# Gates put into token order by a product on chip instead of a trip through DRAM, in a three-stage kernel whose instruction order is planned by hand

## Chip, core and metric

One core of a Trainium2 chip. The metric is the device time of one execution in microseconds, median over the runs shown.

## The reference, cut to what matters

```python
def reference(...):
    attn_out = _attn_ref(q, k, v)            # 4 batches, 8 heads, 576 tokens, 64 wide; 32 landmarks a head
    x = attn_out.transpose(0, 2, 1, 3).reshape(2304, 512)
    x = _moe_ref(x, ...)                     # router, one expert a token, gate_w[token] * (relu(x @ w1[e]) @ w2[e])
    return _moe2_ref(x, ...)                 # rms norm * rms_g, silu(xn @ w_gate) * (xn @ w_val) @ w_out

def _attn_ref(q, k, v):                      # Nystrom attention: out = A @ Z @ C @ v
    q_lm, k_lm = means of 18 neighbouring tokens
    A, Bm, C = sm(q, k_lm), sm(q_lm, k_lm), sm(q_lm, k)
    Z = Bm.T / (norm1 * norminf + 1e-6); six times Z = 2 * Z - Z @ Bm @ Z

def _moe_ref(x, expert_emb, tau, w1, w2):
    logits = (x / |x|) @ (expert_emb / |expert_emb|).T / tau
    expert_idx = argmax(logits); gate_w = softmax(logits)[expert_idx]
```

## The kernel before, in words

The work is one program with three stages that overlap. **Front** (`phaseA`): for each batch b, q and k are loaded (`load`, L241), turned (`turn`), summed into landmarks (`sums`, L267, on VectorE or, as a halving tree of adds, on GpSimd), and go through `crow`, `inverse` (L378), `arow`, `logits`, which ends with the batch's expert index (token `e0`), and `xtile`, which gives each token's sum of squares `ss`. **Expert** (`class Expert`): once `e0` is known the weights of that expert are loaded (`load`, L877, eight 512 KB tiles `raw` in five slots). `first` (L926) multiplies w1 by the low-rank factor, and `rows` evicts the result through ScalarE and VectorE. `hidden` (L960) makes the hidden rows in PSUM banks of which five are to be had; `relu` (L970 on ScalarE, L972 on VectorE) evicts them. `split` (L899, L902) makes f16 pairs of w2 from `raw`. `second` (L999) multiplies by w2; the last 64 tokens of a batch are folded by one product (`fold`, L1008, after a ScalarE copy at L1014), and `out` (L1029, L1033) stores rows to the DRAM tensor `yd`. **Last** (`phase3`): token tiles are read back from `yd` (`prep3`, L1260), normed, combined, transposed by DMA, and multiplied by w_gate, w_val (L1507) and w_out (L1482); these weights come through `W3` (loads of 512 KB at L1166, conversions on VectorE at L1182 to L1186, ScalarE at L1213).

All engines work through a fixed order. `Order` (L28) makes it while the program is written: each task is a generator that yields (engine, cost) or a wait; of the tasks that could go, the one with the earliest start (plus a penalty) is emitted, and its result counts as ready after its cost and the engine's `LAT`. For a DMA (`D`) that is the cost in the yield, 1.5 for an expert load, and 0.95 on top. On the chip every engine then runs its own list strictly in that order and waits on semaphores. Where PE would be idle in the front's plan, `warm` (L227) writes filler products on ones (L236) there. SP issues all DMAs but two.

The gates (`gates`, L804): a chain of small VectorE operations over all 20 columns (4 batches, 5 columns of 128 tokens; the fifth holds 64, in partitions 64 to 127) with one Exp gives `t`. The last stage needs the same values as [128, 18], tokens in tiles of 128 over the whole 2304. That relaying is done through DRAM by six DMAs on SP:

```python
    for b in range(B):
        nc.sync.dma_start(d[b, 0:512].rearrange("(c p) -> p c", p=128), g[:, b, 0:4])       # L848
    nc.sync.dma_start(d[:, 512:576].rearrange("b p -> p b"), g[64:128, :, 4])               # L849
    yield "D", 2.0
    nc.sync.dma_start(st["gam"], st["gd"].rearrange("(t p) -> p t", p=128))                 # L851
```

`embed` (L716) norms the eight expert embeddings in 17 VectorE operations on 8x1 and is added with rank -1 (ahead of all, L778); `inverse` waits for its result (`ent`) just ahead of the product `pen` (L478).

Of the kernel before, what the change touches and what calls it, by code (L numbers as in the profile page):

```python
# [27 lines left out]
class Order:  # L28
# [6 lines left out]

    LAT = dict(P=0.1, V=0.14, W=0.14, A=0.18, G=0.1, D=0.95)

# [41 lines left out]
    def run(self):  # L79
        while self.tasks:  # L80
            now = []
            before = self.tasks[:]
            for t in before:
                kind, arg = t[3]
                while kind in ("wait", "get", "beside", "mark"):
                    if kind == "mark":
                        pass
                    elif kind == "beside":
                        t[1] = t[4]
                    elif kind == "wait":  # L90
                        if arg not in self.tok:
                            break
                        t[1] = max(t[1], self.tok[arg])
                    else:
                        if not self.pool[arg]:
                            break
                        self.pool[arg].sort()
                        t[1] = max(t[1], self.pool[arg].pop(0))
                    t[3] = next(t[2], None)
                    if t[3] is None:  # L100
                        self.tasks.remove(t)
                        break
                    kind, arg = t[3]
                else:
                    costs = arg if len(kind) > 1 else (arg,)
                    _, e, c = min((self.at(e, t[1]) + c + self.pen.get(e, 0) * c, e, c) for e, c in zip(kind, costs))
                    now.append((self.at(e, t[1]), t[0], t, e, c))
# [38 lines left out]
def consts(tc, st):  # L146
    nc = tc.nc
# [25 lines left out]
    st["fold"] = con.tile([128, 64], F32, name="fold")  # L173
    nc.vector.tensor_tensor(out=st["fold"], in0=st["idn"][:, 0:64], in1=st["idn"][:, 64:128], op=ALU.add)
    st["oh"] = con.tile([128, B, 5, 8], F16, name="oh")
    st["WTb"] = st["p2"].tile([128, B, 2, 2, 64], F32, name="WTb")
# [11 lines left out]
def phaseA(tc, ctx, c2, I, st, Jobs):  # L188
# [13 lines left out]
    bufs = dict(q=2, k=2, v=1, kT=2, qT=3, ts=2, kq=4, ct=2, et=4, raw=5, w2p=6, Pt=1, hT=8, etp=4, y=2)  # L202
    R = Order(dict(bufs, ae=2, ce=2, big=1, t=NPT, m=NPM, n=0, r=RB, e=EB, x=1, y2=2, rows=2), dict(P=0.5, V=1.5, A=3.8, G=2.3, D=1.75), PEN)
    wes = [p1.tile([128, 2, 32], F32, name=f"We{i}") for i in range(2)]
# [36 lines left out]
    def load(b, hh, src):  # L241
        yield "get", src
        yield "D", 1.65
        t = T[src, b, hh] = sb([128, 18, 64], src)
        nc.sync.dma_start(t, I[src][b, 4 * hh:4 * hh + 4].rearrange("h (l j) d -> (h l) j d", j=18))
        R.sig(src, b, hh)

    def loadv(b):
        yield "get", "v"
        yield "D", 3.6  # L250
        t = T["v", b] = sb([128, 8, 5, 64], "v")
        nc.sync.dma_start(t[:, :, 0:4].rearrange("p h c d -> p h (c d)"), I["v"][b, :, 0:512, :].rearrange("h (s c) d -> s h (c d)", c=4))
        nc.sync.dma_start(t[0:64, :, 4], I["v"][b, :, 512:576, :].rearrange("h s d -> s h d"))
        R.sig("v", b)
# [12 lines left out]
    def sums(b, hh, i, src):  # L267
# [5 lines left out]
        g = T[src + "T", b, hh][:, :, -576:].rearrange("p e (l j) -> p e l j", j=18)  # L273
        yield ("VG", (1.45, 3.3)) if b < 2 else ("G", 3.3)
        if R.eng != "G":
# [102 lines left out]
    def inverse(b):  # L378
# [73 lines left out]
        V.tensor_copy(Y, pp) if R.eng == "V" else A.copy(Y, pp)  # L452
        R.put("t")
        yield "get", "t"
        yield "P", 0.44
        pwt = ps_t.tile([128, 2, 2, 32], F32, name="pwt", tag="t")
        for g in range(2):
            bd = bdm[:, g].rearrange("p (a c) l -> p c a l", c=2)
            for c in range(2):
                nc.tensor.matmul(pwt[64 * c:64 * c + 64, g], lhsT=Y[:, g], rhs=bd[:, c], start=True, stop=True)  # L460
        yield "get", "t"
        yield "P", 0.38
        pw = ps_t.tile([128, 2, 64], F32, name="pw", tag="t")
        for g, h in heads:
            nc.tensor.matmul(pw[h, g], lhsT=Bm[h, g], rhs=Y[h, g], start=True, stop=True)
        WTb = st["WTb"][:, b]
# [4 lines left out]
        R.sig("WTb", b)  # L471
        yield "wait", ("ent",)
        yield "get", "t"
# [8 lines left out]
        R.put("t")  # L482
        R.sig("W", b)
        for g in range(2):
            yield "beside", 0
            yield "V", 0.41
            W = T["W", b, g] = sb([128, 256], "W", 4)
            V.tensor_tensor(out=W.rearrange("p (h d) -> p h d", h=4), in0=bc(pw[:, g], [128, 4, 64], "out"), in1=bc(icm[:, g], [128, 4, 64], "in"), op=ALU.mult)
# [208 lines left out]
    def pair(b):  # L697
# [4 lines left out]
        for hh in range(2):  # L702
# [6 lines left out]
            R.sig("etp", b, hh)  # L709
        yield "D", 0.7  # L710
        nc.sync.dma_start(st["ed"][b], tp)
        yield "wait", ("WTb", b)
        yield "D", 0.4
        nc.sync.dma_start(st["wd"][b], st["WTb"][:, b])
# [62 lines left out]

    R.add(embed(), -1)  # L778
    for b in range(B):
# [24 lines left out]
def gates(tc, R, st):  # L804
# [38 lines left out]
    V.tensor_tensor(out=t.rearrange("p (b c) -> p b c", b=B), in0=t.rearrange("p (b c) -> p b c", b=B), in1=bc(st["rsx"], [128, B, 5], "in"), op=ALU.mult)  # L843
    yield "D", 2.0
    g = t.rearrange("p (b c) -> p b c", b=B)
    d = st["gd"].rearrange("(b s) -> b s", b=B)
    for b in range(B):
        nc.sync.dma_start(d[b, 0:512].rearrange("(c p) -> p c", p=128), g[:, b, 0:4])  # L848
    nc.sync.dma_start(d[:, 512:576].rearrange("b p -> p b"), g[64:128, :, 4])  # L849
    yield "D", 2.0  # L850
    nc.sync.dma_start(st["gam"], st["gd"].rearrange("(t p) -> p t", p=128))  # L851
    yield "W", 0.18
# [4 lines left out]
class Expert:  # L857
# [19 lines left out]
    def load(self, b):  # L877
# [4 lines left out]
        for m in (1, 2):  # L882
            src = self.I[f"moe_w{m}"][bass.ds(e0, 1)].rearrange("a (k p) f -> p (a k) f", p=128)
            for k in range(4):
                yield "get", "raw"
                yield "D", 1.5
                raw = T["raw", m, b, k] = self.tile("raw", [128, m, 1024 // m], F32)
                nc.sync.dma_start(raw, src[:, m * k:m * k + m])
                R.sig("raw", m, b, k)
# [118 lines left out]
    def fold(self, b, pz):  # L1008
# [5 lines left out]
        nc.scalar.copy(y, pz)  # L1014
        R.put("m")
        yield "get", "m"
        yield "P", 0.85
        pz = self.ps.tile([128, 512], F32, name="pz", tag="m")
# [4 lines left out]
    def out(self, b, c, pz, r0, n):  # L1023
# [6 lines left out]
        R.put("m")  # L1030
        yield "D", 0.73
        t0 = 576 * b + 128 * c
# [213 lines left out]
def prep3(nc, R, stg, st, p):  # L1246
# [6 lines left out]
    def load(k):  # L1253
# [3 lines left out]
        yield "get", "y2"  # L1257
        yield "D", 0.73
        y = ys[k] = stg.tile([128, 512], F32, name="y2", bufs=2)
# [26 lines left out]
    for j in range(h):  # L1286
# [22 lines left out]
        for a in range(2):  # L1309
            yield "D", 1.57  # L1310
            nc.sync.dma_start_transpose(out=st["xT"][XT[p]][:, a, :, 128 * j:128 * j + 128], in_=rows[a].rearrange("p o d -> p (o d)"))
            R.put("rows")
# [25 lines left out]
def phase3(tc, ctx, I, st, out, stg, w3, R=None):  # L1338
# [86 lines left out]
    def last(p, t, g, po):  # L1425
# [15 lines left out]
        if g < 5:  # L1441
            return
        yield "D", 0.73
        n = PT[p][t]
# [74 lines left out]
def loads(R, w3):  # L1519
    while w3.nload < len(w3.jobs):  # L1520
        yield "get", "r"
        yield "D", 1.46
        w3.load()
# [10 lines left out]
def build(tc, I, out):  # L1534
    nc = tc.nc
    with ExitStack() as ctx:
# [6 lines left out]
        st["yd"] = dr.tile([NT, DM], F32, name="yd")  # L1543
        st["gd"] = dr.tile([NT], F32, name="gd")
        st["wd"] = dr.tile([B, 128, 2, 2, 64], F32, name="wd")
# [69 lines left out]
```

## Time and profile before

| | us |
|---|---|
| median of 3 runs | 719.98 (718.86 to 722.33) |
| the profiled execution | 716.13 |
| its span, first to last instruction | 714.4 |
| mean granted TensorE clock | 0.99 of full |
| PE busy | 682.7 |
| VectorE (DVE) busy | 456.0 |
| ScalarE (ACT) busy | 365.2 |
| GpSimd (POOL) busy | 69.6 |

Busy times are of the one profiled execution, and shares of them are averages over stages. The clock is given as a share of 2.4 GHz. An engine's idle time before an instruction is written in brackets with what released it.

### The profile page before, as it was taken

The numbers are of one execution on the slowest core, as the hardware profiler recorded it, in microseconds if no ns is written. First come the engines' busy times: TensorE is split into PE (matmuls) and PEld (weight loads), VectorE is DVE, ScalarE is ACT, GpSimd is POOL, SyncE is SP. The second block draws the span as 40 slices with busy tenths as digits, with TensorE's granted clock in tenths as the row PEclk, the third lists the DMA queues.
The fourth block names the chain that finished last, engine by engine and source line by source line (L and its number), as shares of the span: only waits on it lengthen the run. The fifth ranks groups of instructions, "written<-read, shape, count | busy, mean of one in ns | idle before, by whom it ended". The sixth has DMA issues, their size and how long they took to land. (4 is left out here: it accounts for less than half of the span.)

```text
span 714.4 us, 14850 instructions
## 1 busy us (share of the span) xinstructions
PE 682.7 (96%) x5996; PEld 474.7 (66%) x5996; DVE 456.0 (64%) x1071; ACT 365.2 (51%) x851; POOL 69.6 (10%) x89
## 2 busy tenths in 40 slices
PE   9989999999679998998999999999999999999994
PEld 9867677655424545466777777777777777777882
DVE  8997886735578887878887955456554543344331
ACT  1335775636446957566466554454544443333431
POOL 0025571010110301000000100000000000000000
PEclk9999999999889999999999999999999999999998
DMA  8255807435776885466313220452422030000101
GB/s 300 94 187 196 269 9 250 141 115 158 126 229 189 241 220 174 147 173 156 108 33 116 89 61 1 96 126 76 115 54 68 18 95 1 1 1 2 61 1 35
DMA packets 70142, 80.91 MB, mean 113 GB/s; under 512 B 42920, under 2 KB 47528, under 8 KB 70064
## 3 DMA queue, kind: packets, MB, share of 16 engines
q1 hardware_dynamic: 70032, 79.86, 38.7%
q8 instruction: 49, 0.80, 0.5%
q14 instruction: 29, 0.24, 0.1%
q10 hardware_dynamic: 32, 0.02, 0.0%
HBM read 59.27 MB, written 12.33 MB: 100 GB/s over the span
## 5 line engine op out<-in xcount | busy, mean ns | idle before, releaser
L1482 PE MATMUL po<-w_out,u 128*128 128x512 f16 x648 | 157.5, 379 | 0.7 <-ACT u L1412 0.5
L1507 PEld LDWEIGHTS <-w_gate 128*128 128x128 f16 x1260 | 114.0, 98 | 35.6 <-issue 2.0
L1507 PEld LDWEIGHTS <-w_val 128*128 128x128 f16 x1260 | 113.5, 98 | 13.0 <-issue 1.5
L1482 PEld LDWEIGHTS <-u 128*128 128x128 f16 x648 | 62.7, 98 | 55.8 <-ACT u L1412 1.5
L1385 DVE SCALAR_TENSOR_TENSOR cgate<-ps_gateb,cgate 128x256 f32<-128x256 f32 x81 | 34.2, 422 | 97.6 <-ACT cgate L1382 94.7
L1507 PE MATMUL ps_gatea<-x,w_gate 128*128 128x256 f16 (+1 forms) x720 | 88.6, 262 | 0.0
L1507 PE MATMUL ps_vala<-x,w_val 128*128 128x256 f16 (+1 forms) x720 | 88.6, 262 | 0.0
L999 PE MATMUL pz<-w2p,hT 128*128 128x512 f16 x384 | 86.8, 380 | 0.0
L1382 ACT ACTIVATE cgate<-ps_gatea 128x256 f32<-128x256 f32 x81 | 31.0, 382 | 96.9 <-PE ps_gatea L1507 96.4
L999 PEld LDWEIGHTS <-hT 128*128 128x128 f16 x384 | 36.0, 98 | 49.3 <-issue 5.7
L1507 PE MATMUL ps_gateb<-x,w_gate 128*128 128x256 f16 (+1 forms) x540 | 66.4, 262 | 1.3 <-DVE cgate L1385 1.3
L1507 PE MATMUL ps_valb<-x,w_val 128*128 128x256 f16 (+1 forms) x540 | 66.4, 262 | 1.0 <-DVE cval L1385 0.7
L960 PE MATMUL ph<-etp,Pt 128*128 128x288 f16 x384 | 52.3, 293 | 6.1 <-DVE hT L972 6.1
L1412 ACT CAST u<-cval 128x512 f16<-128x512 f32 x54 | 33.3, 616 | 41.6 <-DVE cval L1391 22.4
L960 PEld LDWEIGHTS <-Pt 128*128 128x128 f16 x384 | 37.9, 100 | 17.6 <-issue 6.6
L1416 DVE TENSOR_TENSOR u<-cval,u 128x512 f16<-128x512 f32 x54 | 37.3, 691 | 16.2 <-ACT u L1412 14.1
L1391 DVE TENSOR_TENSOR cval<-cval,cgate 128x256 f32<-128x256 f32 x81 | 35.3, 436 | 8.7 <-ACT cgate L1388 1.0
L1382 ACT ACTIVATE cval<-ps_vala 128x256 f32<-128x256 f32 x81 | 31.0, 383 | 16.7 <-PE ps_vala L1507 16.5
L1385 DVE SCALAR_TENSOR_TENSOR cval<-ps_valb,cval 128x256 f32<-128x256 f32 x81 | 34.0, 420 | 8.6 <-ACT cval L1382 8.0
L1388 ACT ACTIVATE cgate<-cgate 128x256 f32<-128x256 f32 x81 | 33.5, 413 | 4.8 <-DVE cgate L1385 4.6
L972 DVE SCALAR_TENSOR_TENSOR hT<-ph,hT 128x288 f16<-128x288 f32 x64 | 27.3, 450 | 6.8 <-ACT hT L970 6.1
L970 ACT ACTIVATE hT<-ph 128x288 f16<-128x288 f32 x64 | 25.1, 409 | 10.5 <-PE ph L960 9.8
(224 smaller groups left out, 936.3 us busy)
## 6 DMA issues: line engine op xcount, KB each, us to landing
raw<-moe_w SPq DMA_DIRECT2D x32, 512.0 KB, 5.2
y<-yd SPq DMA_DIRECT2D x36, 256.0 KB, 3.4
r<-moe_w_gate SPq DMA_DIRECT2D x12, 512.0 KB, 4.6
r<-moe_w_val SPq DMA_DIRECT2D x12, 512.0 KB, 3.7
r<-moe_w_out SPq DMA_DIRECT2D x12, 512.0 KB, 3.6
k<-k SPq DMA_DIRECT2D x8, 576.0 KB, 4.9
q<-q SPq DMA_DIRECT2D x8, 576.0 KB, 5.4
out<-o SPq DMA_DIRECT2D x18, 256.0 KB, 2.0
```

The source lines that it names most:

```text
L960: nc.tensor.matmul(ph, lhsT=P[:, g, a, 128 * j:128 * j + 128], rhs=x[:, g, c, 288 * n:288 * n + 288], start=(q == 0), stop=(q == 5))
L970: nc.scalar.activation(h[:, 0, sl], ph, AF.Relu)
L972: nc.vector.scalar_tensor_tensor(out=h[:, 1, sl], in0=ph, scalar=0.0, in1=h[:, 0, sl], op0=ALU.max, op1=ALU.subtract)
L999: nc.tensor.matmul(pz, lhsT=h[:, a, s0:s0 + n], rhs=w[:, e, i], start=(j == 0 and q == 0), stop=(j == 6 and q == 5))
L1382: return lambda: (start(nm) if (i, h) == (1, 0) else None, A.activation(c[nm][:, i, h], banks[nm + ab][:, 0:m], AF.Copy, scale=C))
L1385: return lambda: V.scalar_tensor_tensor(out=c[nm][:, i, h], in0=banks[nm + "b"][:, 0:m], scalar=C, in1=c[nm][:, i, h], op0=ALU.mult, op1=A ...
L1388: return lambda: A.activation(c["gate"][:, i, h], c["gate"][:, i, h], AF.Silu)
L1391: return lambda: either(nc, R).tensor_tensor(out=c["val"][:, i, h], in0=c["val"][:, i, h], in1=c["gate"][:, i, h], op=ALU.mult)
L1412: A.copy(u[0][:, 0, i], c["val"][:, i].rearrange("p h m -> p (h m)"))
L1416: return lambda: either(nc, R).tensor_tensor(out=u[0][:, 1, i], in0=c["val"][:, i].rearrange("p h m -> p (h m)"), in1=u[0][:, 0, i], op=AL ...
L1482: nc.tensor.matmul(po[t], lhsT=u2[:, a, i, 128 * s:128 * s + 128], rhs=wo[:, b, i], start=(first and i == 0 and j == 0), stop=(final and i ...
L1507: nc.tensor.matmul(o, lhsT=wt[:, a, kk, w, 128 * (g % 2):128 * (g % 2) + 128], rhs=xT[:, b, 2 * x + kk, 0:m], start=(first and q == 0), st ...
```

## The change

Six things: the gates are relaid by one product with a matrix that swaps the halves of the partitions, and five VectorE copies, so that the six DMAs and `gd` are gone; `embed` has the rank of `inverse` and a penalty; `inverse` waits for `ent` ahead of `pwt` and makes `pw` after `We`; one landmark sum (batch 0, second half, q) goes to GpSimd; the planner counts a DMA's landing as 1.6 instead of 0.95, with higher costs for most DMAs; and `fold` gets a lag of 1.0 in the plan and a cost of 0.5 instead of 0.85.

```diff
-    LAT = dict(P=0.1, V=0.14, W=0.14, A=0.18, G=0.1, D=0.95)
+    LAT = dict(P=0.1, V=0.14, W=0.14, A=0.18, G=0.1, D=1.6)
...
+                    elif kind == "lag":
+                        t[1] += arg
...
+    st["swap"] = con.tile([128, 128], F32, name="swap")
+    for h in range(2):
+        nc.vector.tensor_copy(st["swap"][:, 64 * h:64 * h + 64], st["idn"][:, 64 - 64 * h:128 - 64 * h])
...
-    R = Order(dict(bufs, ...), dict(P=0.5, V=1.5, A=3.8, G=2.3, D=1.75), PEN)
+    R = Order(dict(bufs, ...), dict(P=0.5, V=1.5, A=3.8, G=2.3, D=0.2), PEN)
...
-        yield "D", 1.65
+        yield "D", 1.89
...
-        yield ("VG", (1.45, 3.3)) if b < 2 else ("G", 3.3)
+        yield ("G", 3.3) if b > 1 or (b, hh, src) == (0, 1, "q") else ("VG", (1.45, 3.3))
...
+        yield "wait", ("ent",)
         yield "get", "t"
         yield "P", 0.44
         pwt = ps_t.tile([128, 2, 2, 32], F32, name="pwt", tag="t")
...
-        yield "get", "t"
-        yield "P", 0.38
-        pw = ps_t.tile([128, 2, 64], F32, name="pw", tag="t")
-        for g, h in heads:
-            nc.tensor.matmul(pw[h, g], lhsT=Bm[h, g], rhs=Y[h, g], start=True, stop=True)
...
-        yield "wait", ("ent",)
...
         R.sig("W", b)
+        yield "get", "t"
+        yield "P", 0.38
+        pw = ps_t.tile([128, 2, 64], F32, name="pw", tag="t")
+        for g, h in heads:
+            nc.tensor.matmul(pw[h, g], lhsT=Bm[h, g], rhs=Y[h, g], start=True, stop=True)
...
-    R.add(embed(), -1)
+    R.add(embed(), PR["inv"], dict(W=0.2, V=0.2))
...
-    yield "D", 2.0
-    g = t.rearrange("p (b c) -> p b c", b=B)
-    d = st["gd"].rearrange("(b s) -> b s", b=B)
-    for b in range(B):
-        nc.sync.dma_start(d[b, 0:512].rearrange("(c p) -> p c", p=128), g[:, b, 0:4])
-    nc.sync.dma_start(d[:, 512:576].rearrange("b p -> p b"), g[64:128, :, 4])
-    yield "D", 2.0
-    nc.sync.dma_start(st["gam"], st["gd"].rearrange("(t p) -> p t", p=128))
+    yield "get", "m"
+    yield "P", 0.2
+    ps = st["ps_m"].tile([128, n], F32, name="psw", tag="m")
+    nc.tensor.matmul(ps, lhsT=st["swap"], rhs=t, start=True, stop=True)
+    g, h = [x.rearrange("p (k o c) -> p k o c", k=2, o=2) for x in (t, ps)]
+    o = st["gam"].rearrange("p (k c) -> p k c", k=2)
+    for to, fr in ((o[:, :, 0:4], g[:, :, 0, 0:4]), (o[64:128, :, 8:9], g[64:128, :, 1, 4:5]), (o[0:64, :, 4:5], h[0:64, :, 0, 4:5]),
+                   (o[64:128, :, 4:8], h[64:128, :, 1, 0:4]), (o[0:64, :, 5:9], h[0:64, :, 1, 0:4])):
+        yield "V", 0.16
+        V.tensor_copy(to, fr)
+        yield "beside", 0
+    R.put("m")
...
-                yield "D", 1.5
+                yield "D", 1.71
...
+        yield "lag", 1.0
         yield "get", "m"
-        yield "P", 0.85
+        yield "P", 0.5
...
-        yield "D", 0.73
+        yield "D", 0.85
...
-        yield "D", 1.46
+        yield "D", 1.71
```

The other costs of DMAs that change: v 3.6 to 3.78, `ed` 0.7 to 1.80, `wd` 0.4 to 0.36, the transposes of `prep3` 1.57 to 1.80; the stores and loads of `yd` and of the output all go from 0.73 to 0.85.

## Rows read from the trace of the kernel before

**Rows 1.** The page, part 1: busy time, share of the span and instructions.

```profile
PE 682.7 (96%) x5996; PEld 474.7 (66%) x5996; DVE 456.0 (64%) x1071; ACT 365.2 (51%) x851; POOL 69.6 (10%) x89
```

**Rows 2.** Stretches: length, busy PE, PEld, DVE, ACT, POOL, clock, DMA share, GB/s.

```profile
180.00:200.00 20.00, 14.24 (x85) 8.63 (x83) 9.78 (x22) 6.91 (x18) 0.39 (x1) 0.83 0.73 129
200.00:220.00 20.00, 15.96 (x67) 6.03 (x65) 17.32 (x42) 12.75 (x23) 2.40 (x3) 0.91 0.78 240
...
360.00:400.00 40.00, 40.00 (x304) 29.51 (x302) 34.41 (x72) 24.55 (x57) 2.83 (x3) 1.00 0.16 54
```

**Rows 3.** PE's timeline: start, us, what; in brackets the idle time before.

```profile
181.09 6.04 PE L960 MATMUL ph<-etp,Pt 128*128 128x288 f16 x48 [0.20 <-DVE hT L972]
192.69 4.48 PE L960 MATMUL ph<-etp,Pt 128*128 128x288 f16 x18 [5.56 <-DVE hT L972]
197.10 2.37 PE L926 MATMUL pP<-raw,WTb 128*64 128x512 f32 x8
199.40 1.47 PE L999 MATMUL pz<-w2p,hT 128*128 128x512 f16 x6
204.91 3.68 PE L926 MATMUL pP<-raw,WTb 128*64 128x512 f32 x8 [4.04 <-DVE Pt L936]
...
244.19 1.94 PE L926 MATMUL pP<-raw,WTb 128*64 128x512 f32 x8
```

**Rows 4.** ScalarE's timeline: the two splits of w2 that waited for a load.

```profile
189.96 1.06 ACT L899 ACTIVATE w2p<-raw 128x1024 f16<-128x1024 f32 x1 [6.05 <-DMA raw<-moe_w]
...
201.51 1.06 ACT L899 ACTIVATE w2p<-raw 128x1024 f16<-128x1024 f32 x1 [5.33 <-DMA raw<-moe_w]
```

**Rows 5.** SP's timeline: DMA issues around the gates.

```profile
180.41 0.39 SPq L888 DMA_DIRECT2D raw<-moe_w  x1
181.88 2.10 SPq L848 DMA_DIRECT2D gd<-gt  x4
...
192.30 0.39 SPq L888 DMA_DIRECT2D raw<-moe_w  x1
```

**Rows 6.** DMA issues: count, KB each, median us to landing, whole span.

```profile
raw<-moe_w SPq DMA_DIRECT2D x32, 512.0 KB, 5.2
...
gd<-gt SPq DMA_DIRECT2D x4, 2.0 KB, 11.3
```

**Rows 7.** The same view for the stretch 180 to 181 us alone.

```profile
raw<-moe_w SPq DMA_DIRECT2D x1, 512.0 KB, 9.5
```

**Rows 8.** A stretch inside the first stall; columns as in rows 2.

```profile
187.00:190.00 3.00, 0.13 (x2) 0.00 (x0) 0.00 (x0) 0.04 (x1) 0.00 (x0) 1.00 0.29 21
```

**Rows 9.** VectorE's timeline near the end of the gates' chain.

```profile
175.28 0.43 DVE L1182 TENSOR_SCALAR e<-r 128x512 int32<-128x512 int32 x1 [1.71 <-DMA r<-moe_w_gate]
...
181.69 0.16 DVE L843 TENSOR_TENSOR gt<-gt,rsx 128x20 f32<-128x20 f32 x1
```

**Rows 10.** VectorE's timeline in the first 20 us.

```profile
4.67 2.22 DVE L263 STREAM_TRANSPOSE kT<-k 128x1152 f32<-128x1152 f32 x1 [1.69 <-DMA k<-k]
6.75 0.15 DVE L730 TENSOR_SCALAR r8i<-ess 8x1 int32<-8x1 int32 x1
...
17.69 0.15 DVE L737 TENSOR_TENSOR r8t<-r8t,ess 8x1 f32<-8x1 f32 x1
17.87 1.35 DVE L276 TENSOR_REDUCE lm<-qT 128x64 f32<-128x1152 f32 x1
```

**Rows 11.** GpSimd's timeline: first and last rows of one landmark sum.

```profile
63.42 1.31 POOL L282 TENSOR_TENSOR ts<-kT 128x576 f32<-128x576 f32 x1 [5.24 <-DVE ev L663]
...
66.57 0.37 POOL L287 TENSOR_TENSOR lm<-ts 128x64 f32<-128x64 f32 x1
```

**Rows 12.** PE groups by line, 20 to 100 us: busy us, mean ns, idle before.

```profile
L236 PE MATMUL w<-ones 128*128 128x128 f16 x194 | 12.9, 219 | 0.0
```

**Rows 13.** PE's timeline: the third fold.

```profile
271.41 1.07 PE L1019 MATMUL pz<-y,fold 128*64 128x512 f32 x2 [2.48 <-ACT y L1014]
```

**Rows 14.** ScalarE's timeline just ahead of that fold's copy.

```profile
270.16 0.63 ACT L1269 ACTIVATE y<-y 128x512 f32<-128x512 f32 x1 [3.96 <-DMA y<-yd]
```

More of the change, by code (lines that the diff above doesn't have):

```diff
@@ L84, in run @@
                 kind, arg = t[3]
-                while kind in ("wait", "get", "beside", "mark"):
+                while kind in ("wait", "get", "beside", "mark", "lag"):
                     if kind == "mark":
                         pass
+                    elif kind == "lag":
+                        t[1] += arg
                     elif kind == "beside":
@@ L202, in phaseA @@
     bufs = dict(q=2, k=2, v=1, kT=2, qT=3, ts=2, kq=4, ct=2, et=4, raw=5, w2p=6, Pt=1, hT=8, etp=4, y=2)
-    R = Order(dict(bufs, ae=2, ce=2, big=1, t=NPT, m=NPM, n=0, r=RB, e=EB, x=1, y2=2, rows=2), dict(P=0.5, V=1.5, A=3.8, G=2.3, D=1.75), PEN)
+    R = Order(dict(bufs, ae=2, ce=2, big=1, t=NPT, m=NPM, n=0, r=RB, e=EB, x=1, y2=2, rows=2), dict(P=0.5, V=1.5, A=3.8, G=2.3, D=0.2), PEN)
     wes = [p1.tile([128, 2, 32], F32, name=f"We{i}") for i in range(2)]
@@ L249, in loadv @@
         yield "get", "v"
-        yield "D", 3.6
+        yield "D", 3.78
         t = T["v", b] = sb([128, 8, 5, 64], "v")
@@ L483, in inverse @@
         R.sig("W", b)
+        yield "get", "t"
[3 more added lines that the diff above has]
+            nc.tensor.matmul(pw[h, g], lhsT=Bm[h, g], rhs=Y[h, g], start=True, stop=True)
         for g in range(2):
-            yield "beside", 0
+            if g:
+                yield "beside", 0
             yield "V", 0.41
@@ L709, in pair @@
             R.sig("etp", b, hh)
-        yield "D", 0.7
+        yield "D", 1.80
         nc.sync.dma_start(st["ed"][b], tp)
         yield "wait", ("WTb", b)
-        yield "D", 0.4
+        yield "D", 0.36
         nc.sync.dma_start(st["wd"][b], st["WTb"][:, b])
@@ L843, in gates @@
     V.tensor_tensor(out=t.rearrange("p (b c) -> p b c", b=B), in0=t.rearrange("p (b c) -> p b c", b=B), in1=bc(st["rsx"], [128, B, 5], "in"), op=ALU.mult)
-    yield "D", 2.0
-    g = t.rearrange("p (b c) -> p b c", b=B)
-    d = st["gd"].rearrange("(b s) -> b s", b=B)
-    for b in range(B):
-        nc.sync.dma_start(d[b, 0:512].rearrange("(c p) -> p c", p=128), g[:, b, 0:4])
-    nc.sync.dma_start(d[:, 512:576].rearrange("b p -> p b"), g[64:128, :, 4])
-    yield "D", 2.0
-    nc.sync.dma_start(st["gam"], st["gd"].rearrange("(t p) -> p t", p=128))
+    yield "get", "m"
[8 more added lines that the diff above has]
+        V.tensor_copy(to, fr)
+        yield "beside", 0
+    R.put("m")
     yield "W", 0.18
@@ L1257, in load @@
         yield "get", "y2"
-        yield "D", 0.73
+        yield "D", 0.85
         y = ys[k] = stg.tile([128, 512], F32, name="y2", bufs=2)
@@ L1309, in prep3 @@
         for a in range(2):
-            yield "D", 1.57
+            yield "D", 1.80
             nc.sync.dma_start_transpose(out=st["xT"][XT[p]][:, a, :, 128 * j:128 * j + 128], in_=rows[a].rearrange("p o d -> p (o d)"))
@@ L1442, in last @@
             return
-        yield "D", 0.73
+        yield "D", 0.85
         n = PT[p][t]
@@ L1543, in build @@
         st["yd"] = dr.tile([NT, DM], F32, name="yd")
-        st["gd"] = dr.tile([NT], F32, name="gd")
         st["wd"] = dr.tile([B, 128, 2, 2, 64], F32, name="wd")
```

## The prediction

> **What bounds the kernel now.** The first view is the page's busy time: PE works 96% of the span [rows 1], so the end is set by PE's list, and a gain must come from PE's idle time, from its slow clock or from its filler products. The second view cuts the span into stretches: PE is busy all the time in the last stage (360 to 400 us is one such stretch, and it stays so to the tail), but from 180 to 220 us it has only 14.24 and 15.96 of 20 us, at a granted clock of 0.83 and 0.91 [rows 2]. That is the worst place behind the start. The third view is PE's timeline there: a stall of 5.56 us ahead of 192.69 and one of 4.04 ahead of 204.91 [rows 3]; between and behind them PE ran on the lower level (1.2 GHz) for a time, seen in the durations: eight L926 products took 3.68 us at 204.91 and 1.94 at 244.19 on the full clock. The bracket names VectorE as releaser, but VectorE waits for ScalarE, and ScalarE's timeline gives the root: two splits of w2 stood 6.05 and 5.33 us for an expert load [rows 4], and everything behind them in ScalarE's list, the relus that free PSUM banks included, stood too. Then SP's timeline: those loads were issued at 180.41 and 192.30, around the four gate stores at 181.88 [rows 5]. An expert load lands after 5.2 us in the median, a gate store of 2 KB takes 11.3 [rows 6]; the load of 180.41 took 9.5 [rows 7], the other 201.51 - 192.30 = 9.2. Between 187 and 190 us the DMA engines moved 21 GB/s, while all four engines stood still [rows 8]. I read this as stores of single four-byte values that clog the rings.
>
> **The gates' stores and load go.** From the end of the 48 L960 products (181.09 + 6.04 = 187.13) to the end of the second L926 (204.91 + 3.68 = 208.59) PE took 21.46 us. Its work in there at full clock is 18 x 6.04/48 = 2.27 for L960, 2 x 1.94 for L926 and 1.47 for L999, together 7.6 [rows 3]. So 13.8 us is the most that can be gained. If the order stays and only the landings fall to 5.2 us: the first load lands at 185.6 instead of 189.96, so its slot frees 4.35 earlier and the second is issued at 187.95; that one lands at 193.15 instead of 201.51, 8.4 us earlier, and the second L926 with it. If its clock stays up too, 3.68 - 1.94 = 1.74 more: 10.1. The new plan counts 1.71 + 1.6 = 3.31 us from issue to landing where it counted 1.5 + 0.95 = 2.45, so it puts a split 0.86 us further behind in ScalarE's list; I add that and take **-11.0**, between 8.4 and 13.8. On SP six issues go, four of them 2.10 us together [rows 5].
>
> The row that speaks against this is the issue time: the first late load went out 1.5 us ahead of the stores and was late all the same. The Trainium skill, DMA: Bandwidth & Descriptors, section Queues, rings and completion order, says that each DMA engine takes descriptors in the order of its ring. By that rule the stores could not hold up a load ahead of them, the first stall would stay, and the sum would be that of the first rival below. Against it stands the 21 GB/s of [rows 8]: had a backlog of large loads been the cause, the engines would have moved much more. I take the stores as the cause of both.
>
> **What comes in their place.** One f32 product over 20 columns on PE. The fold is the nearest row: 1.07 us for 512 columns [rows 13]; so between 0 and 1.07, and I take **+0.4**, as most of its columns are missing. It waits for the end of the gates' chain (181.69 + 0.16 [rows 9]), and behind it in PE's list stand the L960 products of batch 1; for those wait the relus. Five copies on VectorE at 0.16 each [rows 9], 0.8 us together, lie where VectorE had 9.78 us of work in 20 [rows 2], so nothing; without that cover they hold up the relu subtractions behind them by 0.8. The swap matrix is two copies at the start, in the 1.69 us in which VectorE waits for the first k [rows 10]: nothing, or 2 x 0.15 by the same short rows if that load came first.
>
> **The head.** Seven of the 17 embedding operations stand between the turns and sums of the first 20 us, the first at 6.75, the last at 17.69, where VectorE is full; each costs its 0.15 and a gap, up to 0.18 (17.69 to 17.87) [rows 10]: 7 x 0.18 = 1.2 us off VectorE's list. At their new rank they fill places where VectorE waits. The sum that goes to GpSimd frees 1.35 us on VectorE [rows 10] and takes 63.42 to 66.94, 3.5 us, there [rows 11]; the landmark comes 3.5 - 1.35 - 1.2 = about 1 us later, but VectorE can turn the next k meanwhile. PE has 12.9 us of fillers between 20 and 100 us [rows 12], so PE waits for this chain, and what VectorE gains there can reach the end. Bounds: +1 (the late landmark decides) and -2.55; I take the embeddings whole and half of the sum, **-1.9**. Putting `pw` behind `We` moves products and adds none: zero; its cover is the same filled stretch, and without it `W` comes late by that one group of products.
>
> **The fold and the longer landings.** The third fold stood 2.48 us [rows 13], because ScalarE ahead of its copy stood 3.96 for a token load [rows 14]. A lag of 1.0 in the plan lets other products go ahead by about that much: between 0 and -2.48, I take **-1.0**. In the rest of the order longer landings move instructions that wait for loads back; I count nothing, with one stall of the size of [rows 13], 2.5 us, either way.
>
> **Sum.** -11.0 + 0.4 - 1.9 - 1.0 = -13.5 us against the profiled execution: 716.1 to 702.6. The median of the runs is 3.9 us above that execution, and the difference should carry over: 719.98 - 13.5 = **706.5**. What a measurement of this kernel can tell from no change is about 0.5%, 3.6 us.
>
> **Rivals.** *Ring order: only the second load was late by the stores.* Then the first stall stays, the second load gains 9.2 - 5.2 = 4.0 and the clock 1.74: -5.7 + 0.4 - 1.9 - 1.0 = -8.2, 711.8. For it: the issue time; against it: [rows 8]. Chance 0.12.
>
> *VectorE becomes the bound ahead of the last stage.* PE comes 13.5 us sooner to the products with w_gate and w_val, while VectorE is at 34.41 of 40 us from 360 to 400 [rows 2] with the weights' conversions. Spare there is 14%; over the 150 us from 210 to 360 that is 21 us, more than 13.5, so it decides only where the spare lies in the wrong places. I price it at half the gain: 719.98 - 6.7 = 713.2. Chance 0.10.
>
> *The loads are late by themselves.* If neither stall came from the stores, the first term is zero: 0.4 - 1.9 - 1.0 = -2.5, 717.5. Against it: of 32 loads these two are far over the median [rows 6, 7]. Chance 0.05.
>
> *PE waits for the gates (slower).* The product stands in PE's list, and the chain ahead of it on VectorE shares its list with conversions that wait for weight loads: 1.71 us at 175.28 is one of three such conversions [rows 9]. Before, PE ran past that; now it stands there. If three loads came as late as the latest one here, 9.5 against 5.2, PE would stand 3 x (9.5 - 5.2) = 12.9 plus the 1.71 of the row and, as after 192.69, run 18 L960 products at half clock for 4.48 - 2.27 = 2.2 more: 16.8, and the gates' term of 11.0 is then no gain either, since the loads are as late as before: 0.4 - 1.9 - 1.0 + 16.8 = +14.3, 734.3. It decides for slower once PE stands over 6.1 us there (2.5 + 3.6). Against it: what made loads that late are, as I read it, the stores that go. Chance 0.05.
>
> **How the numbers follow.** The forecast has 0.68. Its best ends give -13.8 - 2.55 - 2.48 = -18.8, 701.2, and with one stall less 699; its worst -8.4 + 1.07 + 1.0 = -6.3, 713.7. The first two rivals lie inside. I give 699 to 715; outside are the last two rivals and a tenth for a new order that is worse or better by more than a stall. Faster by over 0.5%: the forecast and the first two rivals, 0.90, less 0.03 for a bad order: 0.87. Within 0.5%: the third rival and that 0.03: 0.08. Slower: 0.05.
>
> **What the changed profile would show.** Right: no stores of gates; no expert load at 9 us; the splits' waits for loads near 2 us or less; PE at 19 us or more in each 20 of that stage and clock 1.0; one short f32 product on PE without a stall ahead of it; the embedding operations behind 18 us; the fold's stall under 1.5. Wrong: a stall of 5 us ahead of the L960 products with ScalarE waiting for an expert load; idle time ahead of the new product; PE waiting for weights at the start of the last stage; more fillers between 20 and 100 us than 12.9.

## The result and the profile after

The changed kernel takes 708.42 us in the median (708.07 to 708.80), against 719.63 (718.86 to 722.33) before: a ratio of 0.983, 95% interval 0.980 to 0.986, or 11.2 us less. Forecast were 13.5 less, 706.5 us, with a range of 699 to 715. The profiled execution took 708.07 us, 8.06 less than the profiled one of before (716.13), which is the quickest of all its runs; why these two differences are not alike is a finding of its own, below.

First the page's busy times after the change. They hardly moved against [rows 1]: the same work, fitted together better.

```profile
PE 682.9 (97%) x6052; PEld 477.9 (68%) x6052; DVE 456.4 (65%) x1071; ACT 362.7 (51%) x850; POOL 76.7 (11%) x102
```

The same stretches as [rows 2], after, with the one from 120 us added.

```profile
120.00:140.00 20.00, 18.10 (x217) 11.14 (x218) 9.11 (x27) 11.98 (x32) 1.28 (x1) 0.91 0.45 161
180.00:200.00 20.00, 18.98 (x126) 11.78 (x125) 16.01 (x33) 15.94 (x33) 0.00 (x0) 1.00 0.64 217
200.00:220.00 20.00, 19.63 (x100) 8.43 (x101) 19.38 (x52) 11.84 (x22) 2.14 (x3) 1.00 0.83 283
360.00:400.00 40.00, 40.00 (x299) 29.16 (x298) 31.35 (x66) 24.56 (x57) 3.72 (x4) 1.00 0.28 93
```

From 180 to 220 us PE now has 18.98 and 19.63 of 20 us, where it had 14.24 and 15.96, and its granted clock is 1.00. The last stage (360 to 400) is full, as before. New is the stretch from 120: PE had 19.55 of 20 there before, at a clock of 1.00, and has 18.10 at 0.91 now.

PE's timeline over the place of [rows 3]: the hidden products of batch 1 (L972), `w1` with `raw` (L938), the new product, then the second products (L1011).

```profile
184.71 12.23 PE L972 MATMUL ph<-etp,Pt 128*128 128x288 f16 x96
196.87 1.94 PE L938 MATMUL pP<-raw,WTb 128*64 128x512 f32 x8
198.73 0.40 PE L855 MATMUL psw<-gt,swap 128*128 128x20 f32 x2
200.37 2.75 PE L1011 MATMUL pz<-w2p,hT 128*128 128x512 f16 x12 [1.24 <-DVE Pt L948]
203.05 1.94 PE L938 MATMUL pP<-raw,WTb 128*64 128x512 f32 x8
204.92 10.32 PE L1011 MATMUL pz<-w2p,hT 128*128 128x512 f16 x47
```

All 96 hidden products run without a stall at full clock. The new product takes 0.40 us and nothing is idle ahead of it. ScalarE's two splits there, which stood 6.05 and 5.33 us in [rows 4]:

```profile
193.30 1.06 ACT L911 ACTIVATE w2p<-raw 128x1024 f16<-128x1024 f32 x1 [0.64 <-DMA raw<-moe_w]
...
199.18 1.06 ACT L911 ACTIVATE w2p<-raw 128x1024 f16<-128x1024 f32 x1
```

The issues of expert loads over the whole span, against 5.2 in [rows 6]; the gates' issues are gone from this list:

```profile
raw<-moe_w SPq DMA_DIRECT2D x32, 512.0 KB, 4.1
```

**Where the time went.** I set marks that both kernels pass: the start of batch 1's hidden products (177.06 before, 184.71 after), the second products behind them (208.52 and 204.92), the start of the last stage (312.71 and 306.72), the end of the span (714.4 and 706.1). Between the marks the times changed by **+7.65, -11.25, -2.4 and -2.3**, -8.3 in all, which is the difference of the two spans. The second stretch holds 126 products after and 118 before: six more second products, which are 1.28 us (twelve take 2.75 in the lines above, six take 1.47 in [rows 3]) and are missing from the third. For like work the second gained 12.5 and the third 1.1. So the middle gained somewhat more than was forecast, and the front lost 7.65 of it again. The two stretches ahead of the second products, before and then after (length, busy PE, PEld, DVE, ACT, POOL, clock, DMA share, GB/s):

```profile
20.00:177.06 157.06, 151.81 (x1896) 105.85 (x1894) 114.00 (x314) 86.38 (x229) 43.00 (x55) 1.00 0.48 157
177.06:208.52 31.46, 21.67 (x120) 11.77 (x118) 18.28 (x36) 16.24 (x35) 4.60 (x4) 0.84 0.76 166
```

```profile
20.00:184.71 164.71, 157.83 (x1955) 110.47 (x1954) 117.07 (x321) 86.25 (x231) 48.42 (x60) 0.99 0.44 146
184.71:204.92 20.21, 18.82 (x127) 11.64 (x126) 17.55 (x40) 13.66 (x31) 2.14 (x3) 1.00 0.73 245
```

In the second stretch PE's idle time fell from 9.79 us (31.46 - 21.67) to 1.39, and its busy time by 2.85, with more products, at the higher clock. In the first, PE is busy 6.0 us longer and idle 1.6 longer (6.88 against 5.25). Of the 6.0, fillers are 4.4: [rows 12], 12.9 us and all before 100 us then, stand at 17.3 for this stretch now.

```profile
L242 PE MATMUL w<-ones 128*128 128x128 f16 x249 | 17.3, 220 | 0.0
```

The one large stall of the front, on PE's timeline, is for an expert load; SP's timeline ahead of it, and SP's waits from 100 to 140 us (in total, times, longest), show what came between:

```profile
117.92 1.07 PE L938 MATMUL pP<-raw,WTb 128*64 128x512 f32 x2
121.90 1.50 PE L938 MATMUL pP<-raw,WTb 128*64 128x512 f32 x2 [2.91 <-DMA raw<-moe_w]
```

```profile
109.36 0.35 SPq L900 DMA_DIRECT2D raw<-moe_w  x1
113.00 0.39 SPq L258 DMA_DIRECT2D v<-v  x1
113.45 0.63 SPq L259 DMA_DIRECT2D v<-v  x1
114.34 13.43 SPq L900 DMA_DIRECT2D raw<-moe_w  x6
```

```profile
SPq L258 <- PE pv L376: 3.2, 1, 3.2
```

SP stood 3.2 us for the one buffer of `v`, which PE's `pv` products still read, and six expert loads stood behind it. That this cost the front its time is a theory until an experiment moves it; the eighth below does.

### The profile page after: what moved, and what is told of

It is laid out like the page before. It is cut to its first block, busy times and chain, and to the rows that moved or that the text cites. A ratio compares the mean times of both kernels' runs of the same rounds, so it can differ in the third digit from the quotient of the medians.

```text
span 706.1 us, 14955 instructions
## 1 busy us (share of the span) xinstructions
PE 682.9 (97%) x6052; PEld 477.9 (68%) x6052; DVE 456.4 (65%) x1071; ACT 362.7 (51%) x850; POOL 76.7 (11%) x102
## 5 line engine op out<-in xcount | busy, mean ns | idle before, releaser
L1011 PE MATMUL pz<-w2p,hT 128*128 128x512 f16 x384 | 87.0, 379 | 1.2 <-DVE Pt L948 1.2
L1011 PEld LDWEIGHTS <-hT 128*128 128x128 f16 x384 | 36.2, 98 | 49.1 <-issue 7.0
L972 PE MATMUL ph<-etp,Pt 128*128 128x288 f16 x384 | 50.1, 286 | 3.1 <-DVE hT L984 2.2
L972 PEld LDWEIGHTS <-Pt 128*128 128x128 f16 x384 | 36.8, 98 | 14.8 <-issue 3.4
L242 PE MATMUL w<-ones 128*128 128x128 f16 x486 | 33.2, 229 | 1.1 <-DVE mask L156 1.1
```

Of the source, the lines that this page charges most:

```text
L242: nc.tensor.matmul(w, lhsT=st["ones"], rhs=st["ones"], start=True, stop=True)
L972: nc.tensor.matmul(ph, lhsT=P[:, g, a, 128 * j:128 * j + 128], rhs=x[:, g, c, 288 * n:288 * n + 288], start=(q == 0), stop=(q == 5))
L1011: nc.tensor.matmul(pz, lhsT=h[:, a, s0:s0 + n], rhs=w[:, e, i], start=(j == 0 and q == 0), stop=(j == 6 and q == 5))
```

## The experiments

Ratios are to runs of the kernel before in the same group: 721.01 us in the median for runs 1, 2, 4 and 5, 721.35 for 6, 7, 8 and the first of run 10, 722.17 for the others. Beside the change it was 719.63. One kernel's median thus moves by 2.5 us from group to group, and a smaller difference between runs of two groups is not told from none. "Front" is the start of batch 1's hidden products in the profile of that run.

**1. The gates alone.** Before, with the product and its five copies, and no other edit.

```diff
-        nc.sync.dma_start(d[b, 0:512].rearrange("(c p) -> p c", p=128), g[:, b, 0:4])
...
-    nc.sync.dma_start(st["gam"], st["gd"].rearrange("(t p) -> p t", p=128))
+    nc.tensor.matmul(ps, lhsT=st["swap"], rhs=t, start=True, stop=True)
...
+        V.tensor_copy(to, fr)
```

> Kernel before with the gates' product and copies alone; plan costs, embeddings, sums and fold as before. Theory (the four-byte gate stores held up both expert loads): the two splits wait under 2.5 us each, no PE stall over 2.5 us from 180 to 210 us, hidden of batch 1 still starts near 177 us, and the time is 9 to 12 us under the kernel before. Rival ring order (only the load issued behind the stores was held up): 4 to 6 us under it. Rival loads late by themselves: within 2 us of it.

Measured: 711.31 us, ratio 0.9855 (0.9805 to 0.9905), 9.7 us less. The splits waited 1.77 and 1.05 us. So most of the whole change's gain is this part. The product came at 230.46 here, far behind the hidden products of batch 1, so the loads recover without it being early.

**2. The same six transfers, by rows.** Before, with the gates stored and loaded as rows of consecutive values, which leaves them out of token order. The list of instructions of every engine is that of before, in the same order.

```diff
-        nc.sync.dma_start(d[b, 0:512].rearrange("(c p) -> p c", p=128), g[:, b, 0:4])
-    nc.sync.dma_start(d[:, 512:576].rearrange("b p -> p b"), g[64:128, :, 4])
+        nc.sync.dma_start(d[:, 4 * b:4 * b + 4], g[:, b, 0:4])
+    nc.sync.dma_start(d[:, 16:18], t[:, 0:2])
...
-    nc.sync.dma_start(st["gam"], st["gd"].rearrange("(t p) -> p t", p=128))
+    nc.sync.dma_start(st["gam"], st["gd"].rearrange("(p c) -> p c", p=128))
```

> Kernel before with the same six DMAs at the same places of every engine's list, but each with one contiguous run a partition (16, 8 and 72 bytes) in place of single four-byte values: about 900 runs instead of 4,600; the gates then are not in token order. Theory (the many four-byte runs clog the rings): a store lands in under 5 us, the split that waited 6.05 us waits under 2.5, the time is 8 to 12 us under the kernel before. Rival ring order: the first split still waits about 6 us, 4 to 6 us under. Rival loads late by themselves: both splits still wait 5 us, within 2 us.

Measured: 708.89 us, 0.9835 (0.9782 to 0.9889). The DMA issues and ScalarE's two splits in this run:

```profile
gd<-gt SPq DMA_DIRECT2D x4, 2.0 KB, 4.1
```

```profile
185.30 1.06 ACT L899 ACTIVATE w2p<-raw 128x1024 f16<-128x1024 f32 x1 [1.73 <-DMA raw<-moe_w]
191.72 1.06 ACT L899 ACTIVATE w2p<-raw 128x1024 f16<-128x1024 f32 x1 [1.61 <-DMA raw<-moe_w]
```

The load that in [rows 7] took 9.5 us, from the stretch 180 to 181 us here, still ahead of the stores:

```profile
raw<-moe_w SPq DMA_DIRECT2D x1, 512.0 KB, 5.2
```

And PE's marks, front and second products, before and then here:

```profile
177.06 3.84 PE L960 MATMUL ph<-etp,Pt 128*128 128x288 f16 x30
208.52 6.65 PE L999 MATMUL pz<-w2p,hT 128*128 128x512 f16 x30
```

```profile
177.04 9.76 PE L960 MATMUL ph<-etp,Pt 128*128 128x288 f16 x78
198.04 14.42 PE L999 MATMUL pz<-w2p,hT 128*128 128x512 f16 x66
```

A store of the same 2 KB lands after 4.1 us where it took 11.3 [rows 6], and both splits wait under 2 us, the first too, whose load is issued ahead of the stores. The second products start at 198.04 instead of 208.52. So neither the number of transfers nor their place but their single four-byte values held the loads up. (By the access patterns the pieces fall from 4,608 to 768, and the trace has 3,840 packets fewer, 66,302 for 70,142; the 900 of the expectation is too many. Whether their number or their size counts, this run does not show.) "Ring order" and "late by themselves" fall here.

**3. Only the stores by rows**, with the load of four-byte values left (the first two lines of the edit above; the gates are out of token order).

> Kernel before with the five gate stores by rows (16 and 8 bytes a partition) and the gate load still in single four-byte values; same order of every engine; the gates are then not in token order. Theory (the stores are what held up both expert loads): both splits wait under 2.5 us, time as with stores and load by rows, 709, within 2 us. Rival (the load of 2,304 four-byte values holds up the second expert load by itself): first split under 2.5 us, the second still 4 to 6 us late, time 712 to 717.

Measured: 710.85 us, 0.9846 (0.98 to 0.9892). The stores are nearly all of it. The first split still waits, longer than the theory had it, which stays open; the second, whose load is issued at 193.93, just ahead of the load of four-byte values at 194.50, does not, so the rival fell:

```profile
191.58 1.06 ACT L899 ACTIVATE w2p<-raw 128x1024 f16<-128x1024 f32 x1 [3.51 <-DMA raw<-moe_w]
197.80 1.06 ACT L899 ACTIVATE w2p<-raw 128x1024 f16<-128x1024 f32 x1
```

This run shows one thing more. PE's, VectorE's, ScalarE's and GpSimd's lists are those of before and of run 2, yet the front came at 181.58, against 177.06 and 177.04. The difference starts at one weight load, here in this run and then in the kernel before:

```profile
77.34 2.90 PE L926 MATMUL pP<-raw,WTb 128*64 128x512 f32 x6 [2.79 <-DMA raw<-moe_w]
```

```profile
74.92 1.93 PE L926 MATMUL pP<-raw,WTb 128*64 128x512 f32 x6 [1.19 <-DMA raw<-moe_w]
```

PE stood longer and then ran the same six products at a lower granted clock (0.82 from 75 to 80 us and 0.84 to 85, in the mean of its two levels), 2.90 us for 1.93. In run 1, whose PE and SP lists are those of before up to the front, the wait was 2.09, the six took 3.61 and the front came at 180.07. So the order of before has a place where executions part by up to 4.5 us, and its profiled execution took the short side, as did that of run 2.

**4. The longer landings alone**, put into before.

```diff
-    LAT = dict(P=0.1, V=0.14, W=0.14, A=0.18, G=0.1, D=0.95)
+    LAT = dict(P=0.1, V=0.14, W=0.14, A=0.18, G=0.1, D=1.6)
...
-                yield "D", 1.5
+                yield "D", 1.71
...
```

> Kernel before with the plan's DMA costs and landing alone (1.6 instead of 0.95 and the costs of the loads). Theory (the new plan's order costs the front about 8 us, between the expert indices of batches 1 and 2): hidden of batch 1 starts 5 to 9 us later than the 177 us of before, the gates' stalls stay, the time is 2 to 9 us over the kernel before. Rival (the front's loss comes from the embeddings' rank, the GpSimd sum and pw behind We): hidden of batch 1 within 2 us of 177, time within 3 us of the kernel before.

Measured: 723.97 us, 1.0038 (1.0013 to 1.0064), 3 us more. The front came at 184.10, as the theory had it, though later by only 2.5 to 7 than the fronts of the order of before (177.04 to 181.58). The gates' stores were issued at 195.60, and PE stood 8.54 us at 219.55, so this stall only moved; the four expert loads issued from 199.95 on, behind the stores, took 18.7 us in the median to land, and 20.4 at most. Another stall of 5.86 came at 253.09.

**5. All but the gates.** The change, with the gates through DRAM again (run 1's edit reversed).

> Changed kernel with the gates through DRAM as before. Theory: front as in the changed kernel (hidden of batch 1 near 185 us), the gates' stall is back: 8 to 12 us over the changed kernel, 717 to 721. Rival (the longer landings in the plan alone would have moved the splits behind the late loads, and the product adds nothing): within 3 us of the changed kernel.

Measured: 720.79 us, 0.9998 (0.9972 to 1.0024), with the front at 186.73. Against the change that is 12.4 us: the gates are worth that in the new order, and all other edits together nothing while the stores stay. The stall is back on PE (3.92 us at 201.85), and a store takes 13.1 us.

**6. The change without the longer landings** (run 4's edit reversed, out of the change).

> Changed kernel with the plan's DMA costs and landing of the kernel before (gates' product, embeddings, sums, pw and fold as changed). Theory (the front's loss of 7 us up to hidden of batch 1 comes from the plan's longer landings): hidden of batch 1 starts at 176 to 179 us instead of 184.7, and if what follows is as in the changed kernel the time is 3 to 7 us under it, 701 to 705. Rival (longer landings cost the front 7 us but save as much behind it, in splits and folds that would wait for loads): within 2 us of the changed kernel, 708. Rival (the loss is from embeddings, sum and pw): hidden of batch 1 at 183 or later.

Measured: 711.0 us, 0.9844 (0.9803 to 0.9884), 2.6 more than the change, about what groups differ by. The front came at 182.88, where the theory had 176 to 179: taking the landings out of the change does not bring the front back, though putting them into before had delayed it (run 4). Other stalls stood there, 2.59 us at 88.64 and 2.17 at 193.43.

**7. Gates and landings**, without the head and the fold.

> Kernel before with the gates' product and the plan's longer landings, embeddings, sums, pw and fold as before. Theory (landings cost the front): hidden of batch 1 at 182 to 187, time 709 to 715, no better than gates only (711.3). Rival (longer landings help where loads are waited for, and it is the embeddings and sums that cost): hidden of batch 1 under 180, time under 707.

Measured: 721.69 us, 0.9997 (0.9972 to 1.0022), which neither side had expected: two parts that give -9.7 and +3.0 alone give nothing together. The gates' gain is there: from the front to the last stage it is 122.3 us, where before takes 135.7 (312.71 - 177.06). But the front came at 186.62, and the last stage is 9.2 us longer than before's: PE stood 4.47 us at 482.98 and 1.70 at 485.07 for transposed tokens, at a clock of 0.74 from 480 to 500. I didn't follow up why they came late.

**8. `v` behind the expert loads.** The change, and batch 3's load of `v` is held back in the plan until the last load of batch 1's first expert weight is issued.

```diff
     def loadv(b):
+        if b == 3:
+            yield "wait", ("raw", 1, 1, 3)
         yield "get", "v"
```

> Changed kernel in which the load of v of batch 3 is put behind the four w1 loads of batch 1 on SP's list. In the changed kernel SP stood 3.1 us for v's slot at 113.0 with those loads behind it, and PE then stood 2.91 us for one of them at 121.9 and ran at the lower clock. Theory (that wait is a large part of the front's loss): no such stall, clock 1.0 from 120 to 140 us, hidden of batch 1 at 179 to 182 instead of 184.7, time 3 to 5 us under the changed kernel. Rival (the front is bound by the chain from expert index to expert index, and the stall only replaces fillers): hidden of batch 1 within 1.5 us of 184.7, time within 2 us.

Measured: **700.53 us** (699.67 to 701.92), 0.9703 (0.9666 to 0.9741): faster than both kernels, and by 7.9 us than the change, more than forecast (before was 1.7 slower in this group, so by the ratios it is 9). SP's timeline, its wait for `v`, and the windows of this run:

```profile
110.10 2.70 SPq L902 DMA_DIRECT2D raw<-moe_w  x5
113.75 0.39 SPq L260 DMA_DIRECT2D v<-v  x1
```

```profile
SPq L260 <- PE pv L378: 0.9, 1, 0.9
```

```profile
20.00:178.95 158.95, 154.15 (x1955) 109.38 (x1953) 117.86 (x322) 86.61 (x231) 48.40 (x60) 1.00 0.46 152
178.95:199.00 20.05, 20.05 (x134) 11.96 (x133) 17.09 (x41) 15.31 (x34) 4.68 (x4) 1.00 0.65 216
120.00:140.00 20.00, 20.00 (x238) 14.18 (x230) 13.84 (x43) 16.47 (x44) 4.18 (x2) 1.00 0.44 147
```

Five expert loads go out in the time in which SP stood for `v`, and `v` itself goes out at 113.75, 0.75 us later than in the change. The front gains 5.76 us (184.71 - 178.95). Up to the front PE is idle 4.80 us instead of 6.88, and busy 154.15 instead of 157.83 with the same number of products. The fillers are 17.3 us in both, so they are no part of it. The place of the stall shows what the rest is made of, in this run and then in the change:

```profile
118.66 1.08 PE L940 MATMUL pP<-raw,WTb 128*64 128x512 f32 x4
123.41 2.21 PE L326 MATMUL pc<-kT,kq 128*128 128x320 f32 x8
```

```profile
128.00 2.21 PE L324 MATMUL pc<-kT,kq 128*128 128x320 f32 x8
```

The windows of the change there:

```profile
120.00:125.00 5.00, 3.10 (x26) 1.37 (x28) 0.95 (x2) 1.56 (x4) 1.28 (x1) 0.74 0.83 320
125.00:130.00 5.00, 5.00 (x66) 3.04 (x65) 1.26 (x3) 2.32 (x6) 0.00 (x0) 0.92 0.41 118
```

Up to these `pc` products PE's list is the same in both kernels. From 118.66 this run takes 4.75 us to them, from 117.92 the change takes 10.08: 5.33 less. Of that, 2.91 is the wait; 1.07 is that four `pP` products run here in one go of 1.08, where the change, with one load late, ran them as two and two (1.07 at 117.92, 1.50 at 121.90); the remaining 1.35 lies where, after the wait, the granted clock was 0.74 and 0.92 in the mean, so for a time on the lower level (1.2 GHz). This run had come to that place 0.74 us later, so 1.2 us more of the front's gain lie behind it. There the plan has put products of PE into another order too, and these 1.2 are not shown to come from the wait.

By the profiled executions this run is 8.40 us quicker. The front is 5.76 of it; from the front to the last stage it takes 118.0 us instead of 122.0, as the change's stalls of 1.24 at 200.37, 1.54 at 237.51 and 0.64 at 245.71 are gone, which the theory did not have; the last stage is 1.4 longer. No stall over 0.3 us is left on PE between 83 and 302 us:

```profile
98.16 0.41 PE L481 MATMUL pen<-ent,WTb 128*64 128x8 f32 x8 [0.26 <-ACT WTb L473]
302.07 0.81 PE L1522 MATMUL ps_gatea<-x,w_gate 128*128 128x256 f16 x6 [2.32 <-ACT cgate L1397]
```

**9. The same without the longer landings** (run 8 with run 4's edit reversed).

> Changed kernel without the longer landings and with v of batch 3 behind the four w1 loads of batch 1. Theory (v ahead of the expert loads was the one cost of the new order, and landings are neutral): within 3 us of the changed kernel with v moved (700.5). Rival (the longer landings are needed for it, as without them splits wait for loads again): a split waits over 2.5 us for a load, and the time is 705 to 712.

Measured: 714.02 us, 0.9891 (0.9846 to 0.9937), 13.5 more than run 8. ScalarE's splits waited 3.18 us at 81.75 and 5.64 at 202.76 for expert loads. So the same edit is worth +3.0 in before, about nothing or a little less in the change (-2.6 between two groups) and -13.5 here.

**10. The lag, added and taken.** Run 1 with the fold's lag:

```diff
+        yield "lag", 1.0
         yield "get", "m"
-        yield "P", 0.85
+        yield "P", 0.5
```

> Kernel before with the gates' product and the fold's lag. Theory: front as in the gates-only kernel (hidden of batch 1 at 180), no stall over 1.5 us ahead of a fold's product, time 0 to 2.5 us under gates only, 709 to 711. Rival (the fold's lag only moves another wait): no difference to gates only, or slower.

Measured: 711.81 us, 0.9853 (0.9804 to 0.9903), no gain over run 1's 711.31. No fold stands, but run 1 has no such stall either (0.11 us at its third fold, 262.56); and one of 5.64 us at 250.45 came. And the change without it:

> Changed kernel with the fold planned as before (no lag, cost 0.85). Theory (the lag takes away a fold's stall of about 2.5 us): one or two of the four fold products stand 2 to 3 us behind ScalarE's copy, time 1 to 3 us over the changed kernel, 709.5 to 711.5. Rival (the lag only shifts the order and other stalls decide): no such stall, or a time outside 707 to 712 for another reason that its trace names.

Measured: 709.66 us, 0.9838 (0.9794 to 0.9883), not told from the change's 0.983, and all four folds start without a stall there too: the theory fell. The stall went with the product of the gates, as run 1 shows; run 2, with the order of before, still has it (2.62 us at 260.92).

**11. The embeddings at their old rank**, in the change.

```diff
-    R.add(embed(), PR["inv"], dict(W=0.2, V=0.2))
+    R.add(embed(), -1)
```

> Changed kernel with the embeddings at their old rank ahead of all. Theory (seven operations at 0.18 us in the full first 20 us of VectorE are a real cost): expert index of batch 0 at 61.2 to 61.9 us instead of 60.5, time 0.5 to 3 us over the changed kernel if the order behind it stays alike. Rival (the head is bound by the loads and by ScalarE and GpSimd, so the rank does nothing there): expert index of batch 0 within 0.3 us of 60.5.

Measured: 709.85 us, 0.983 (0.9784 to 0.9877), the same ratio as the change's. Batch 0's expert index started at 61.44 us instead of 60.46, so the rank is worth about 1 us at that mark, in one profile each; in the time it does not show.

## Why the prediction was right, and where not

**The gates (-11.0 + 0.4): right, in mechanism and size.** The stretch from the front to the second products fell by 11.25 us, and by 10.5 in run 2 with nothing but the form of the transfers changed (208.52 to 198.04, from fronts that agree to 0.02); for that, the order kept, the prediction had worked out 10.1. The doubtful step, taking the stores as the cause of both late loads against the issue time, holds by run 2. The 0.86 us that it added for the new plan is not shown by any run. Alone (9.7 us) and within the rest (12.4) the part lies around the forecast. In the profiles of the three kernels with stores of single values (before, runs 4 and 5) the way from the front to the last stage takes 133.9 to 137.0 us, in the eleven others 118.0 to 128.8. The product cost 0.40 us, the value taken, and the copies nothing that shows; the 1.24 behind the product is a wait for `Pt`, which was not in the sum.

**The rivals.** *Ring order* and *late by themselves* fell by run 2. What the prediction held against the latter, that of 32 loads these two are far over the median, was weaker than it looked: before has loads of 9.5 us at 76.1 and 9.2 at 112.6 with no gate stores near, and the change one of 8.9 at 115.6, against the sign "no expert load at 9 us". A long landing alone does not tell of the stores; the same load at 5.2 us in run 2 does. *PE waits for the gates*: nothing idle ahead of the product at 198.73. *VectorE becomes the bound*: PE stood 1.16 us for `cval` at 312.78, and the last stage was 2.3 us shorter, not longer.

**The fold (-1.0): the right sign for a wrong reason.** The stall of 2.48 [rows 13] is gone, but by runs 1 and 10 the lag isn't what removed it. The stretch that holds it is 2.4 us shorter, 1.28 of that by the six products that moved ahead of its mark; PE's idle time in it fell by only 1.2 (3.56 to 2.36), as the stalls at 237.51 and 245.71 came.

**The head (-1.9): mis-sized.** Batch 0's expert index came at 60.46 us instead of 61.05, 0.6 earlier. The embeddings are worth about what the step said (1.0 by run 11 against 1.2); half of the sum's 1.35 did not show (with the embeddings at their old rank the index came at 61.44, later than before's 61.05), and the fillers, which were to give time back, grew: 15.5 us between 20 and 100 us, where 12.9 was named as the bound for right.

**The step that failed** is "In the rest of the order longer landings move instructions that wait for loads back; I count nothing, with one stall of the size of [rows 13], 2.5 us, either way". The front lost 7.65 us between the profiled executions (3.1 of it against the front of run 3, whose list is that of before). Run 8 got 5.76 of it back by moving one load that waited at the head of SP's list: 5.33 at the stall itself, where the price was not its length alone (2.91 us) but 2.4 more for products that ran in two goes and at a lower clock. The landings are not the whole cause by themselves: put into before they delay the front (184.10 and 186.62 in runs 4 and 7), but taken out of the change they leave it at 182.88. I costed a fresh order as if it were the old one with small shifts; each of the orders tried has fronts between 177 and 187 us and stalls in places of its own.

**The median.** "The difference should carry over" failed too, to the good. The 3.9 us between the profiled execution of before and its median were taken as the same in both kernels. Run 3 shows a place in the old order where executions part by 4.5 us, and the profiled one was on its short side; that the other executions of before lie on the long side fits their spread (718.4 to 725.9 over the three groups; the change's four lie within 0.8) but I have no profiles of them. So -8.06 by the profiles became -11.2 by the medians. That this lies within 2.3 us of the forecast is thus in part luck: by the profiles, which the sum was made for, it was -8.06 for -13.5, and 3.1 us that the sum did not have stood against the front's loss, which it did not have either.

**Left open:** why the last stage is 2.3 us shorter, why the first split of run 3 still waits 3.51, and why runs 6, 7 and 9 pay where they do.

## What to carry to other kernels

Keep transfers of single four-byte values away from large loads that something waits for, or give them rows: here they cost ten microseconds, on loads issued ahead of them too. When a fixed order is made anew, compare it stage by stage with marks that both kernels pass; a gain of 11 us in one stage hid a loss of 7.65 in another, and two lines got 5.76 back. Compare it with several executions of the old order, too. On a queue that issues in order, look for what stands behind a transfer that waits for its buffer.

## What was not expected of the hardware

A load of 512 KB that was issued 1.5 us ahead of stores of 2 KB was held up by them: 9.5 us [rows 7], its split waiting 6.05, against 5.2 and 1.73 with the same stores by rows (run 2). Loads issued behind such stores took up to 20.4 us (run 4). The Trainium skill, DMA: Bandwidth & Descriptors, section Queues, rings and completion order, has each DMA engine take descriptors in the order of its ring. From that the prediction concluded that later stores could not delay the load; the section does not say so, as by the same sentence a later descriptor may finish its write before an earlier one. The trace does not agree with the conclusion, and the measurement decides; by which path the stores reach the earlier load, no run here shows.

A short stall cost more than its length: at 77.34 us in run 3, 2.79 us of waiting were followed by six products at 2.90 us instead of 1.93, and in the change the 2.91 us at 121.90 by 2.4 more, 1.35 of them where the granted clock had fallen (0.91 in the mean of 120 to 140 us).
